# Units 6 and 7 of an attention-and-MLP kernel: transposes from TensorE to the DMA queue, loads issued behind them

## The chip, the cores and the metric

One core of a Trainium2 chip. The metric is the time of one execution in microseconds (us), the median over executions. Most executions of one kernel agree within 0.3%. All times inside a trace are microseconds from the start of the profiled span, and the span is about 1.7 us shorter than the time.

## The reference

A recurrent attention over 4 batches, 8 heads, 768 steps and a head width of 48; its output, as 3072 rows of 384, goes through two matrix layers with a SiLU between them.

```
for t in range(S):                                   # S = 768
    cur = einsum('bhd,bhe->bhde', u * k[t], v[t])
    y[t] = einsum('bhd,bhde->bhe', r[t], state + cur)
    state = w * state + einsum('bhd,bhe->bhde', k[t], v[t])
x = y as rows of (batch, step), columns of (head, d)   # 3072 x 384
h = x @ w_in                                           # 384 x 2048
out = (h * sigmoid(h)) @ w_out                         # 2048 x 384
```

## The kernel before

The sequence is cut into 6 chunks of 128 steps. A unit is one chunk of one batch, so there are 24 units: units 4 to 7 are chunk 1. Per unit, TensorE makes the scores (`p2`), the output y (`p3y`) and the state sums; VectorE adds the bonus term and writes y as 16-bit (`p3e`); `p4` turns y so that its columns lie on partitions, into xT, which layer one reads. Layers one and two (`l1`, `l2`) are cut into pieces, "fillers", and `fill(n)` puts some of them between the attention steps, so that TensorE always has work. Each engine runs its instructions in the order in which they are written.

```python
def p4(i):                                   # before
    ...
    if i >= 2 * B:                           # units 8 to 23: DMA transpose on the SyncE queue
        nc.sync.dma_start_transpose(out=xts[sc][:, :, b, :], in_=L["y16"]...)
        return
    yT = ps.tile(...)                        # units 0 to 7: three TensorE transposes,
    for q in range(NQ):
        nc.tensor.transpose(yT[:, q, :], yf[:, 128*q:128*q + 128], ident16)
    nc.scalar.copy(out=xts[sc][:, :, b, :], in_=yT)    # and a ScalarE copy out of PSUM

for i in range(B + 2, NU):                   # units 6 to 23; B = 4, NIN = 6
    ...                                      # p2(i), fill(2), front(i + 1)
    if NIN <= i < 2 * B:
        load(i + NIN)                        # i = 6, 7: loads of units 12, 13
    fill(1)
    p3y(i); p3e(i)
    ...                                      # sums, state
    fill(2)
    p4(i)
    if i >= 2 * B:
        load(i + NIN)
    ...
    fill(1)
    ...
    if b == B - 1:                           # after unit 7:
        if sc == 1:
            fillers.extend(l1s(1, 2, 4) + l2s(1))   # layer one over units 6 and 7
```

`load` issues three DMAs (r, k, v; 192 KB each) on the SyncE queue, the same queue that carries the DMA transposes and the output stores.

Of the kernel before, what the change touches and what calls it, by code (L numbers as in the profile page):

```python
# [15 lines left out]
def kernel(  # L16
# [13 lines left out]
    B, H, S, D = r.shape  # L30
# [10 lines left out]
    NIN = 6  # L41
# [19 lines left out]
    def unit(i):  # L61
        return divmod(i, B)

    def load(i, mid=None):
        if i >= NU:
            return
        sc, b = unit(i)
        for t, src in ((rin, r), (kin, k), (vin, v)):
            if t is vin and mid:
                mid()  # L70
            nc.sync.dma_start(out=t[i % NIN][:, :, 0:D],
                              in_=src[b, :, sc * C:sc * C + C, :]
                              .rearrange("h t d -> t h d"))
# [120 lines left out]
    def bonus_sum(i):  # L194
        L = live[i]
        L["rku"] = wrk.tile([128, H], FP, name="rku", bufs=3)
        nc.vector.tensor_reduce(out=L["rku"], in_=L["rku_f"], axis=mybir.AxisListType.X,  # L197
                                op=ALU.add)

    def bonus_vu(i):  # L200
        L = live[i]
        L["vu"] = wrk.tile([128, H, D], FP, name="vu", bufs=3)
        nc.gpsimd.tensor_tensor(out=L["vu"], in0=vin[i % NIN],  # L203
                                in1=L["rku"].unsqueeze(2).broadcast_to([128, H, D]),
                                op=ALU.mult)
# [50 lines left out]
    def r16(i):  # L256
        L = live[i]
        L["rT16"] = wrk.tile([PR, NP, C], F16, name="rT16")
        nc.scalar.copy(out=L["rT16"], in_=L["rT"])  # L259

    def p2(i, spins=0, nxt=None, late=False):
        L = live[i]
        ae = ps.tile([128, NP, C], FP, name="ae", tag="t", bufs=5)
        ao = ps.tile([128, NP, C], FP, name="ao", tag="t", bufs=5)
        spin(spins, ae)
        for p in range(NP):
            nc.tensor.matmul(ae[:, p, :], L["kT"][0:D, p, :], L["rT"][0:D, p, :],  # L267
                             start=True, stop=True)
            nc.tensor.matmul(ao[:, p, :], L["kT"][64:PR, p, :], L["rT"][64:PR, p, :],  # L269
                             start=True, stop=True)  # L270
        if nxt is not None:
            p1t(nxt)
        L["am"] = []
        for a in (ae, ao):
            am = wrk.tile([128, NP, C], F16, name="am", bufs=4)
            nc.vector.tensor_tensor(out=am, in0=a,  # L276
                                    in1=maskM.unsqueeze(1).broadcast_to([128, NP, C]),
                                    op=ALU.mult)
            L["am"].append(am)
        if nxt is not None and not late:  # L280
            p1d(nxt)

    def p3y(i):
        sc, b = unit(i)
        L = live[i]
        v16 = L["v16"]
        L["y"] = y = ps.tile([128, H, D], FP, name="y", tag="t", bufs=5)
        for p in range(NP):
            if sc:
                nc.tensor.matmul(y[:, 2 * p:2 * p + 2, :], L["rT16"][:, p, :],  # L290
                                 st16[b][:, p, :], start=True, stop=False)
            for j in range(2):
                nc.tensor.matmul(y[:, 2 * p + j, :], L["am"][j][:, p, :],  # L293
                                 v16[:, 2 * p + j, :], start=not sc,
                                 stop=(not sc or j == 1))

    def p3e(i):
        L = live[i]
        L["y16"] = wrk.tile([128, H, D], F16, name="y16", bufs=3)
        nc.vector.tensor_tensor(out=L["y16"], in0=L["y"], in1=L["vu"], op=ALU.add)  # L300

    def sums(i):
        sc, b = unit(i)
        L = live[i]
        L["sps"] = sps = ps.tile([128, NP, PW], FP, name="sps", tag="t", bufs=5)
        kf = kc[i % NKC].rearrange("p h d -> p (h d)")
        vf = L["v16"].rearrange("p h d -> p (h d)")
        for p in range(NP):
            nc.tensor.matmul(sps[:, p, :], kf[:, 128 * p:128 * p + 128],  # L309
                             vf[:, PW * p:PW * p + PW], start=True, stop=True)  # L310

    def state(i):
        sc, b = unit(i)
        sps = live[i]["sps"]
        for p0, c0 in ((0, 0), (64, D)):
            dst = st[b][p0:p0 + D, :, c0:c0 + D]
            if sc:
                nc.vector.tensor_tensor(out=dst, in0=sps[p0:p0 + D, :, c0:c0 + D],  # L318
                                        in1=sdec[b][p0:p0 + D, :, c0:c0 + D], op=ALU.add)
            else:  # L320
                nc.vector.tensor_copy(out=dst, in_=sps[p0:p0 + D, :, c0:c0 + D])
        if sc > 1:
            nc.gpsimd.tensor_copy(out=st16[b], in_=st[b])  # L323
        if sc < NCH - 2:
            nc.gpsimd.tensor_tensor(out=sdec[b], in0=st[b],  # L325
                                    in1=wCT.unsqueeze(2).broadcast_to([PR, NP, PW]),
                                    op=ALU.mult)

    def half_state(b):
        nc.scalar.copy(out=st16[b], in_=st[b])  # L330
# [3 lines left out]
    def p4(i):  # L334
        sc, b = unit(i)
        L = live[i]
        if sc not in xts:
            xts[sc] = wrk.tile([128, NQ, B, C], F16, name="xT", bufs=3)
        if i >= 2 * B:
            nc.sync.dma_start_transpose(out=xts[sc][:, :, b, :],  # L340
                                        in_=L["y16"].rearrange("p h d -> p (h d)"))
            return
        yT = ps.tile([128, NQ, C], F16, name="yT", tag="t", bufs=5)
        yf = L["y16"].rearrange("p h d -> p (h d)")
        for q in range(NQ):
            nc.tensor.transpose(yT[:, q, :], yf[:, 128 * q:128 * q + 128], ident16)  # L346
        nc.scalar.copy(out=xts[sc][:, :, b, :], in_=yT)
# [43 lines left out]
    def l1s(sc, b0=0, b1=B):  # L391
        return [((b1 - b0) / B, lambda ft=ft: l1(sc, ft, b0, b1)) for ft in range(NFT)]

    def l2s(sc, b0=0, b1=B):
        return [(1.0, lambda b=b, part=part: l2(sc, b, part))
                for b in range(b0, b1) for part in range(4)]
# [4 lines left out]
    def fill(n):  # L401
        owed[0] = min(owed[0] + n, n + 1.0)
        while fillers and owed[0] > 0.01:
            w_, f = fillers.pop(0)
            owed[0] -= w_
            f()
# [48 lines left out]
    p3e(1)  # L455
    spin(1)
    p4(0)
    p1(2)
    nat_ku(2)
# [5 lines left out]
    load(B)  # L465
    load(B + 1)
    p4(1)
    nc.scalar.copy(out=st[2], in_=zero)
    spin(2)
# [9 lines left out]
    p1(3)  # L479
    fill(1)  # L480
    p4(2)
    nat_ku(3)
    nat_rk(3)
# [20 lines left out]
    def front(i):  # L504
        nat_v(i)
        nat_ku(i)
        nat_rk(i)
        nat_kc(i)
# [63 lines left out]
    for i in range(B + 2, NU):  # L572
        sc, b = unit(i)
        if i == B + 2:
            p2(i, nxt=i + 1)
        bonus_sum(i)
        bonus_vu(i)
        if i > B + 2:
            p2(i, nxt=i + 1 if i + 1 < NU else None)
        fill(2)  # L580
        if i + 1 < NU:
            front(i + 1)
        if NIN <= i < 2 * B:
            load(i + NIN)
        fill(1)
        p3y(i)
        p3e(i)
        if sc < NCH - 1:
            sums(i)
            state(i)  # L590
        fill(2)
        p4(i)
        if i >= 2 * B:
            load(i + NIN)
        if i + 1 < NU:
            r16(i + 1)
        if i == B + 2:
            half_state(3)
        fill(1)
        if sc == 1:  # L600
            half_state(b)
        fill(1 if sc in (2, 3) else 2)
        if b == B - 1:
            if sc == 1:
                fillers.extend(l1s(1, 2, 4) + l2s(1))
            else:
                fillers.extend(l1s(sc) + l2s(sc))
# [32 lines left out]
```

## Time and profile before

| | before |
|---|---|
| time, median of 3 | 199.74 us (199.5 to 199.87) |
| profiled span | 197.8 us |
| TensorE busy | 189.7 us, 96% |
| DMA transposes | 16, median 2.4 us from issue to landing |
| granted TensorE clock | 1.000 |

The page gives the busy shares and the DMA load over the span; the timeline of one engine gives each group of instructions as start, duration, engine, source line, operation, output<-input, count, and in brackets how long the engine stood idle before it and what ended that. The lines that matter are in the prediction. Three more are needed later, all TensorE: the layer-one pieces just before unit 6's transposes, the start of layer two behind them, and the layer-two pieces just before the tile that the prediction calls the deadline.

```profile
45.53 1.47 PE L358 MATMUL hps<-xT,win 128*128 128x256 f16 x12
...
48.35 1.46 PE L370 MATMUL ops<-wout,gT 128*128 128x384 f16 x8
...
61.37 2.11 PE L370 MATMUL ops<-wout,gT 128*128 128x384 f16 x12
```

From 61.37 to the deadline tile at 63.32 are 1.95 us for twelve matmuls. There is no wait in it, so 1.95 us is the yardstick for that stretch in every other trace.

### The profile page before, as it was taken

To read this page: it belongs to the slowest core of one execution; us is meant where nothing else is said; L and a number is where in the kernel's file an instruction comes from. 1 tells how busy PE (TensorE), PEld (TensorE's weight loads), DVE (VectorE), ACT (ScalarE), POOL (GpSimd) and SP (SyncE) were. 2 spreads that over 40 slices of the span, in tenths; PEclk is the share of its full clock that TensorE was granted. 3 is DMA by queue.
4 is the path that set the end of the run, shared out by engine and by line. 5 is a ranking of instruction groups with operands and counts; after the bars stand their busy time and mean duration, and the time that the engine had idled before them with its cause. 6 is when DMAs were issued, how large, how long until landed. Compare 5 with 4: busy or idle time off the path is not lost.

```text
span 197.8 us, 4932 instructions
## 1 busy us (share of the span) xinstructions
PE 189.7 (96%) x1925; PEld 127.2 (64%) x1925; DVE 115.4 (58%) x233; ACT 91.9 (46%) x209; POOL 115.1 (58%) x145
## 2 busy tenths in 40 slices
PE   7889999998999999999999999999999999999993
PEld 2657878787766976675566766557656556544562
DVE  6687658885758746975575686466576344210121
ACT  3565487798232652215961216682015680069300
POOL 4499959979956795697669647735537710000000
PEclk9999999999999999999999999999999999999999
DMA  4999998999899883766456387520321011310022
GB/s 85 209 185 171 198 227 167 166 187 195 162 193 215 209 168 84 171 137 157 91 119 139 99 182 159 103 59 5 101 60 43 20 22 43 97 42 0 3 80 81
DMA packets 88864, 23.92 MB, mean 121 GB/s; under 512 B 82056, under 2 KB 88840, under 8 KB 88840
## 3 DMA queue, kind: packets, MB, share of 16 engines
q1 hardware_dynamic: 85160, 20.46, 48.0%
q0 software_dynamic: 3680, 3.15, 10.8%
q8 instruction: 15, 0.25, 0.5%
q14 instruction: 9, 0.07, 0.1%
HBM read 20.45 MB, written 4.72 MB: 127 GB/s over the span
## 4 chain that ended last, share of the span: by engine, by line
PE 82%; issue 5%; POOL 5%; DVE 4%; ACT 2%; POOLq 0%; DVEq 0%
PE ops L370 31%; PE hps L358 27%; PE ae L267 10%; PE xs L242 4%; PE y L293 3%; DVE am L276 2%; PE y L290 2%; POOL ku L180 2%; PE ops L384 1%; PE sps L309 1%; POOL rku_f L186 1%; PE yT L346 1%; ACT gT L361 1%; DVE y L300 1%; PE ao L269 1%
## 5 line engine op out<-in xcount | busy, mean ns | idle before, releaser
L361 ACT ACTIVATE gT<-hps 128x256 f16<-128x256 f32 (+1 forms) x128 | 59.7, 493 | 46.7 <-PE hps L358 45.0
L358 PE MATMUL hps<-xT,win 128*128 128x256 f16 (+1 forms) x384 | 69.4, 326 | 0.5 <-ACT gT L361 0.3
L370 PE MATMUL ops<-wout,gT 128*128 128x384 f16 x368 | 64.0, 327 | 0.0
L358 PEld LDWEIGHTS <-win 128*128 128x128 f16 x384 | 35.4, 98 | 23.3 <-issue 1.2
L370 PEld LDWEIGHTS <-gT 128*128 128x128 f16 x368 | 34.5, 98 | 22.3
L276 DVE TENSOR_TENSOR am<-ae,maskM 128x512 f16<-128x512 f32 x24 | 16.6, 691 | 36.2 <-PE ao L269 36.2
L374 DVE COPY osb<-ops 128x384 f32<-128x384 f32 x23 | 12.7, 554 | 27.5 <-PE ops L370 27.4
L267 PE MATMUL ae<-rk 48*128 48x128 f32 x192 | 27.7, 285 | 0.7 <-DVE rk L230 0.7
L267 PEld LDWEIGHTS ae<-rk 48*128 48x128 f32 x192 | 23.1, 187 | 8.1 <-issue 4.5
L269 PE MATMUL ao<-rk 48*128 48x128 f32 x192 | 27.7, 285 | 0.0
L259 ACT CAST rT<-rk 112x512 f16<-112x512 f32 x20 | 12.3, 616 | 32.1 <-DVE rk L253 32.1
L203 POOL TENSOR_TENSOR vu<-vin,rku 128x384 f32<-128x384 f32 x23 | 19.1, 830 | 13.8 <-DVE rku L197 13.7
L253 DVE TENSOR_TENSOR rk<-xs,pif 112x512 f32<-112x512 f32 x40 | 25.6, 681 | 1.7 <-PE xs L242 1.7
L186 POOL TENSOR_TENSOR rku_f<-rin,ku 128x384 f32<-128x384 f32 x24 | 24.1, 1006 | 1.9
L180 POOL TENSOR_TENSOR ku<-kin,u_bc 128x384 f32<-128x384 f32 x24 | 24.1, 1005 | 1.5 <-DMA kin<-in_k_dram 1.5
L191 POOL TENSOR_TENSOR kc<-kin,lamC 128x384 f16<-128x384 f32 x24 | 24.1, 1004 | 0.0
L269 PEld LDWEIGHTS ao<-rk 48*128 48x128 f32 x192 | 23.2, 187 | 0.0
L323 POOL CAST stb<-st 112x384 f16<-112x384 f32 x12 | 6.0, 503 | 22.2 <-DVE st L318 22.2
L300 DVE TENSOR_TENSOR y<-y,vu 128x384 f16<-128x384 f32 x24 | 13.4, 557 | 7.6 <-PE y L293 3.2
L276 DVE TENSOR_TENSOR am<-ao,maskM 128x512 f16<-128x512 f32 x24 | 16.3, 680 | 0.0
L325 POOL TENSOR_TENSOR sdec<-st,pif 112x384 f32<-112x384 f32 x16 | 13.3, 836 | 1.8 <-ACT gT L361 1.1
L197 DVE TENSOR_REDUCE rku<-rku_f 128x8 f32<-128x384 f32 x24 | 13.2, 549 | 2.0 <-POOL rku_f L186 1.6
(74 smaller groups left out, 171.0 us busy)
## 6 DMA issues: line engine op xcount, KB each, us to landing
rin<-in_r_dram SPq DMA_DIRECT2D x24, 192.0 KB, 3.6
kin<-in_k_dram SPq DMA_DIRECT2D x24, 192.0 KB, 3.4
vin<-in_v_dram SPq DMA_DIRECT2D x24, 192.0 KB, 3.6
out_dram<-osb SPq DMA_DIRECT2D x23, 192.0 KB, 1.9
win<-in_moe_w_in_dram POOLq DMA_DIRECT2D x4, 384.0 KB, 5.7
wout<-in_moe_w_out_dram POOLq DMA_DIRECT2D x2, 768.0 KB, 11.3
xT<-y SPq DMA_TRANSPOSE x16, 2.4
out_dram<-osh SPq DMA_DIRECT2D x1, 128.0 KB, 1.8
```

The source lines that it names most:

```text
L180: nc.gpsimd.tensor_tensor(out=L["ku"], in0=kin[i % NIN][:, :, 0:D], in1=u_bc, op=ALU.mult)
L186: nc.gpsimd.tensor_tensor(out=L["rku_f"], in0=rin[i % NIN][:, :, 0:D], in1=L["ku"], op=ALU.mult)
L191: nc.gpsimd.tensor_tensor(out=kc[i % NKC][:, :, 0:D], in0=kin[n][:, :, 0:D], in1=lamC, op=ALU.mult)
L203: nc.gpsimd.tensor_tensor(out=L["vu"], in0=vin[i % NIN], in1=L["rku"].unsqueeze(2).broadcast_to([128, H, D]), op=ALU.mult)
L253: nc.vector.tensor_tensor(out=rk[:, :, :, 64 * g:64 * g + 64], in0=xs[g][0:PR], in1=lam(g), op=ALU.mult)
L267: nc.tensor.matmul(ae[:, p, :], L["kT"][0:D, p, :], L["rT"][0:D, p, :], start=True, stop=True)
L269: nc.tensor.matmul(ao[:, p, :], L["kT"][64:PR, p, :], L["rT"][64:PR, p, :], start=True, stop=True)
L276: nc.vector.tensor_tensor(out=am, in0=a, in1=maskM.unsqueeze(1).broadcast_to([128, NP, C]), op=ALU.mult)
L300: nc.vector.tensor_tensor(out=L["y16"], in0=L["y"], in1=L["vu"], op=ALU.add)
L358: nc.tensor.matmul(hps, win[:, q, ft * 128:(ft + 1) * 128], xts[sc][:, q, b0:b1, :].rearrange("p b t -> p (b t)"), start=(q == 0), stop=(q ...
L361: nc.scalar.activation(out=gts[sc][:, ft, b0 * C:b1 * C], in_=hps, func=AF.Silu)
L370: nc.tensor.matmul(ops, gts[sc][:, ft, b * C:(b + 1) * C], wout[:, ft, :], start=(ft == 0), stop=(ft == NFT - 1))
```

## The change

The intent is to take two units' transposes off the engine that is full. Their slot loads go behind the transposes on the queue, so that the transposes need not stand behind them.

```diff
@@ p4
-        if i >= 2 * B:
+        if i >= NIN:
             nc.sync.dma_start_transpose(...)
@@ the loop over units 6 to 23
-        if NIN <= i < 2 * B:
-            load(i + NIN)
         fill(1)
         p3y(i)
...
         p4(i)
-        if i >= 2 * B:
+        if i >= NIN:
             load(i + NIN)
```

## The prediction

> **What bounds the kernel now.** I read the page from the top: busy shares, then the slices, then the chain. All times are microseconds from the start of the profiled span.
>
> ```profile
> span 197.8 us, 4932 instructions
> PE 189.7 (96%) x1925; PEld 127.2 (64%) x1925; DVE 115.4 (58%) x233; ACT 91.9 (46%) x209; POOL 115.1 (58%) x145
> ...
> PE   7889999998999999999999999999999999999993
> ...
> DMA  4999998999899883766456387520321011310022
> ...
> PE 82%; issue 5%; POOL 5%; DVE 4%; ACT 2%; POOLq 0%; DVEq 0%
> ```
>
> TensorE is busy 96% of the span and is 82% of the chain that ended last, so a microsecond gained or lost in TensorE's own order is gained or lost at the end, unless a later wait swallows it. The DMA row is full over the first third (slices of 4.95 us, so up to about 70 us). That is where the change lies: units 6 and 7 are the third and fourth units of the second chunk (units 4 to 7), at about 42 to 57 us. So I read the timeline of each engine from 38 to 66 us. First TensorE, at the two transposes that go, and at the first layer-one matmul behind the second layer of chunk 0:
>
> ```profile
> 47.52 0.34 PE L346 MATMUL yT<-ident,y 128*128 128x128 f16 x3 [0.51 <-DVE y L300]
> 47.70 0.82 PE L358 MATMUL hps<-xT,win 128*128 128x256 f16 x6
> ...
> 55.10 0.33 PE L346 MATMUL yT<-ident,y 128*128 128x128 f16 x3
> 55.27 2.11 PE L370 MATMUL ops<-wout,gT 128*128 128x384 f16 x12
> ...
> 63.32 0.82 PE L358 MATMUL hps<-xT,win 128*128 128x256 f16 x6
> ```
>
> What to see: unit 6's transposes hold TensorE for 0.51 us waiting for VectorE's y, then take 0.18 us of issue (47.52 to 47.70). Unit 7's come without a wait and take 0.17 us (55.10 to 55.27). The chain of waits also runs through here: from 40.65 to 47.52 it goes over POOL and the VectorE addition, the last place but two short ones before the end where TensorE waits for another engine.
>
> The row at 63.32 is the deadline. By the source, the work pushed at the end of unit 7 is layer one of chunk 1 for units 6 and 7, and it stands behind layer one for units 4 and 5 and all of layer two of chunk 0. The 256-wide rows at 63.32 are its first two tiles. They read both units' columns of xT, so **both transposes must have landed by then**.
>
> Now the queue on which the new transposes are issued:
>
> ```profile
> 52.95 0.75 SPq L71 DMA_DIRECT2D rin<-in_r_dram  x1
> 53.80 0.74 SPq L71 DMA_DIRECT2D kin<-in_k_dram  x1
> 54.63 0.67 SPq L71 DMA_DIRECT2D vin<-in_v_dram  x1
> 55.41 0.84 SPq L71 DMA_DIRECT2D rin<-in_r_dram  x1
> 56.33 1.81 SPq L71 DMA_DIRECT2D kin<-in_k_dram  x1
> 58.24 0.72 SPq L71 DMA_DIRECT2D vin<-in_v_dram  x1
> 59.06 0.60 SPq L376 DMA_DIRECT2D out_dram<-osb  x1
> 59.77 0.37 SPq L71 DMA_DIRECT2D rin<-in_r_dram  x1
> ...
> 63.87 1.31 SPq L340 DMA_TRANSPOSE xT<-y  x1
> ```
>
> Counting the triples from the start, the one at 52.95 loads unit 11, 55.41 unit 12, 59.77 unit 13; 63.87 is the transpose of unit 8. The queue issues without a gap: it is in arrears. Unit 12's load is written before unit 6's matmuls end, at about 45 us, yet issues at 55.41. The arrears come from 36 to 50 us, when unit 9's three loads took 5.23, 4.84 and 3.58 us to issue beside the weight transfer of 768 KB.
>
> **What the Trainium skill says.** "VectorE: DVE Perf Modes", section "The three transpose paths", lists 390 ns on TensorE against 1309 ns by DMA for a 128x128 16-bit transpose. The trace agrees in direction only: a TensorE transpose here shows 219 to 231 ns, and in a stream three of them cost 0.17 us; a DMA transpose of three such blocks shows 1.18 to 1.82 us of issue and 2.3 to 4.5 us to landing. So the DMA path is longer, but costs TensorE nothing unless awaited. "DMA: Bandwidth & Descriptors", section "Anatomy of one DMA", says that a DMA's semaphore wait happens on the issuing sequencer before dispatch. The listing agrees: on this queue a DMA that is not ready, or an issue that is slow, delays all behind it. "Perfetto Trace Analysis", section "Identifying the Most-Contended Engine", warns that matmul busy share is no measure of the distance to the peak. It applies: the weight loads are at 64%. Hence I count TensorE's gains by distances between starts and not by the busy times of 0.33 us.
>
> **The change part by part.**
>
> Removed from TensorE: 0.51 + 0.18 us at unit 6, 0.17 us at unit 7, sum 0.86 us. It is on the path, and I see no wait that takes its place between 47 and 62 us: the layer-two weights' second half, issued at 37.78 with 12.3 us to landing, is there at 50.1 against a use at about 50.6 (51.28 less 0.69); the masked scores of unit 7 are ready at 52.22 against a use at 53.25, and move with TensorE. So the deadline moves from 63.32 to 62.46.
>
> Removed from ScalarE: two copies at 0.48 us. Beside other work: in this stretch it waits 4.7 us before one of them. Worth nothing. Also two of the rotating PSUM buffers' uses go; no TensorE wait here is for one.
>
> Added on the queue, unit 6: its y is ready at 47.46, but its place is behind unit 11's load, so it issues at about 55.4, for 1.3 us (like unit 8's), and lands by 58 to 60, well before 62.46. It pushes everything behind it. If issue time binds, by 1.3 us; if DMA throughput binds, by its bytes: 96 KB at the 0.2 MB/us of this stretch, about 0.5 us.
>
> Added, unit 7: its y is ready at 54.46, earlier by 0.69 with TensorE. Its place is behind unit 12's load and the first output store, because the load of unit 12 moves only just behind unit 6's transpose. Those two end at 59.67 now, so it issues at 59.67 + 0.1 + (0.5 to 1.3) = 60.2 to 61.0. Time to landing: unit 8's, in the same traffic, shows 2.7; unit 9's, behind a congested load, 4.5. So it lands between 62.9 and 65.5, most likely 63.2 to 64.5. Against 62.46 that is a **new TensorE wait of 0.4 to 3.0 us, about 1.3**.
>
> Moved: the loads of units 12 and 13, later by about 1 to 3 us. Unit 12 is turned at about 85 us and unit 13 later, over 20 us after landing. Worth nothing. Unit 8's transpose and the stores move by 2 to 3 us, and unit 8's is not read until chunk 2's layer one at 87.65.
>
> Sum: -0.86 + 1.3 = +0.4 us. The new wait lies inside the stretch where TensorE is otherwise full, so later work does not absorb it, save perhaps 0.2 us at 70.88, where TensorE now waits 0.28 us for ScalarE. I put the time at **200.1 us**.
>
> **The rivals.**
>
> Hidden anyway: if unit 7's transpose lands before 62.46, only the gain remains, 199.74 - 0.86 = 198.9 us. For it: the queue may be limited by throughput, and the issue of 1.81 us at 56.33 has slack that the transpose might use. Against it: the arithmetic above reaches 62.9 at best.
>
> Long wait: crowded DMA engines give the 4.5 us landing and the queue slips by the full 1.3 us or more: wait 3 us, time 202 us. For it: the DMA row is at 9 in these slices and some issues on the queue take 1.8 us or more. Against it: unit 8's 2.7 us right behind a load and two stores.
>
> False dependency: unit 6's transpose writes a tile whose other columns TensorE is still reading, at 47.70. If the order were kept for the whole tile, TensorE would stand from 47 to 58 us, 11 us, and the time would be near 210 us. Against it: in the trace the matmuls from 47.70 to 48.52 run over the ScalarE copy into the same tile (47.90 to 48.38), so columns are told apart.
>
> Nearer the weight landing: if the waits of POOL come back, TensorE gains less than 0.69 at unit 6, which costs up to half a microsecond.
>
> **Range and chances.** Hidden anyway has about 0.25, the middle case 0.55, the long wait 0.17, the false dependency 0.03. That gives a range from 198.8 to 201.8 us, with 0.2% between executions. Two per cent is 4 us; only the false dependency or an unforeseen stall reaches it. Faster by over 2% would need 4 us out of parts that hold 0.86.
>
> **What would show each step.** The 0.51 us gap before unit 6's transposes is gone and layer one goes on at about 47.0. There are 18 DMA transposes; the first issues at about 55.4, the second at 60 to 61. At about 62.5 the first 256-wide layer-one tile behind layer two waits for the DMA transpose, 0.4 to 3 us; this is the step I am least sure of. No wait for loads appears near 85 us. The prediction is wrong if the first transpose issues much before or after 55.4, if TensorE waits between 47 and 62 us for something new, or if the later layers lose or gain time that this account does not hold.

## The result, and the profile after

| | before | after |
|---|---|---|
| time, median of 6 each | 199.52 us (199.26 to 199.87) | 198.93 us (198.31 to 199.31) |
| ratio | | 0.9963 (0.9941 to 0.9984) |
| profiled span | 197.8 us | 197.4 us |

A ratio here and below is the mean time of one kernel's fast runs over that of the other's of the same rounds, so not quite the ratio of the medians. Where I turn a ratio into microseconds I multiply its distance from 1 by the median of before in those rounds: here -0.74 us, interval -1.18 to -0.32. The change made the kernel slightly faster, where the prediction had it 0.36 us slower.

The page of the changed kernel:

```profile
span 197.4 us, 4920 instructions
...
PE 190.3 (96%) x1919; PEld 127.8 (65%) x1919; DVE 115.5 (59%) x233; ACT 91.0 (46%) x207; POOL 115.0 (58%) x145
...
PE 83%; DVE 5%; issue 4%; POOL 3%; ACT 1%; DMA 1%; POOLq 0%; DVEq 0%
```

TensorE's busy time did not fall although six transposes left it: a reminder that this sum measures overlapping windows. The new entry is DMA in the chain, 1%. The TensorE timeline shows where it comes from:

```profile
45.80 2.13 PE L358 MATMUL hps<-xT,win 128*128 128x256 f16 x18
47.76 1.46 PE L370 MATMUL ops<-wout,gT 128*128 128x384 f16 x8
...
60.62 2.11 PE L370 MATMUL ops<-wout,gT 128*128 128x384 f16 x12
63.23 0.81 PE L358 MATMUL hps<-xT,win 128*128 128x256 f16 x6 [0.50 <-DMA xT<-y]
```

At the top, the twelve and six layer-one matmuls that unit 6's transposes had parted now run as one group of 18. The start of that group to the start of layer two is 1.96 us, against 2.82 us before (45.53 to 48.35): **0.86 us gained**. At the bottom, the deadline tile starts 2.61 us after its predecessor, 0.66 us over the yardstick: **the new wait**. The bracket says 0.50 because the profile counts idle time from the modelled end of the last matmul. The queue:

```profile
54.20 0.75 SPq L71 DMA_DIRECT2D vin<-in_v_dram  x1
55.05 1.74 SPq L340 DMA_TRANSPOSE xT<-y  x1
56.89 0.51 SPq L71 DMA_DIRECT2D rin<-in_r_dram  x1
57.49 0.54 SPq L71 DMA_DIRECT2D kin<-in_k_dram  x1
58.14 1.61 SPq L71 DMA_DIRECT2D vin<-in_v_dram  x1
59.84 0.85 SPq L376 DMA_DIRECT2D out_dram<-osb  x1
60.78 1.20 SPq L340 DMA_TRANSPOSE xT<-y  x1
```

Unit 6's transpose issues at 55.05, then unit 12's load, one store, and unit 7's transpose at 60.78. TensorE goes on 2.45 us after that issue, at 63.23.

### The profile page after: what moved, and what is told of

The parts are those of the page before. It is cut to its first block, busy times and chain, and to the rows that moved or that the text cites. A ratio compares the mean times of both kernels' runs of the same rounds, so it can differ in the third digit from the quotient of the medians.

```text
span 197.4 us, 4920 instructions
## 1 busy us (share of the span) xinstructions
PE 190.3 (96%) x1919; PEld 127.8 (65%) x1919; DVE 115.5 (59%) x233; ACT 91.0 (46%) x207; POOL 115.0 (58%) x145
## 4 chain that ended last, share of the span: by engine, by line
PE 83%; DVE 5%; issue 4%; POOL 3%; ACT 1%; DMA 1%; POOLq 0%; DVEq 0%
PE hps L358 30%; PE ops L370 29%; PE ae L267 11%; PE xs L242 4%; PE y L293 3%; DVE am L276 2%; PE y L290 2%; PE sps L309 1%; PE ops L384 1%; DMA xT<-y 1%; POOL rku_f L186 1%; POOL ku L180 1%; ACT gT L361 1%; PE yT L346 1%; PE ao L269 1%
```

## The experiments

Theory A: TensorE's gain is what the starts show (0.86 us at unit 6, 0.17 us at unit 7), less a wait for unit 7's transpose that its place on the queue makes. Theory B: executions as a rule have no such wait and the first trace was an accident. Theory C: the transpose's own landing makes the wait, wherever it stands. Every run of the eleven gave correct results.

To compare traces that start differently, I use three starts in each: the first scores of unit 4 (30.10 us in before), the deadline tile (63.32) and the last VectorE copy (194.58). "Middle" is the distance from the first to the second, less before's 33.22 us. "End" is from the last copy to the end of the span, which the trace gives to a thousandth (197.847 in before). What lies between the tile and the last copy takes 131.26 or 131.27 us in every trace of the account below, so nothing is lost or gained there. The stretch before unit 4's scores is left out: the program is the same there in every kernel, and it scatters from 29.82 to 30.74 us.

### The changed kernel again, and the place of the loads

No edit in the first run.

> The changed kernel once more, for a second trace and a narrower interval. Theory A (gain counted by starts, 0.86 us at unit 6 and 0.17 us at unit 7, less a wait for unit 7's DMA transpose that varies from execution to execution): 0.3 to 0.8 us faster than before, and a TensorE wait for the DMA transpose of 0.2 to 1.0 us in this trace. Theory B (the wait in the first trace was an accident, and executions as a rule have none): about 1.0 us faster, and no such wait.

198.99 us, ratio 0.9956 (0.9936 to 0.9975), -0.88 us. The profiled execution was a freak of 489 us and gives no trace: TensorE's layer-two matmuls took a mean of 687 ns there, against 326 ns in the first trace. It was the only such execution, and is left out of the ratio; its cause stays open. The other five lie between 198.26 and 199.20 us. For traces, two more looks were taken:

> The changed kernel, one look for another trace (the trace of the last repeat fell on an execution of 489 us). Theory A: TensorE waits for unit 7's DMA transpose by 0.2 to 1.0 us between starts at the first 256-wide layer-one tile behind layer two; the transpose issues at 60 to 61.5 us. Theory B (no wait as a rule): no such wait.

> The same as again2, once more: both looks together say whether the wait of the first trace was an accident. Theory A: a wait again, of a size that differs by some tenths of a microsecond.

The TensorE timelines around the deadline tile, again2 and then again3:

```profile
60.28 2.11 PE L370 MATMUL ops<-wout,gT 128*128 128x384 f16 x12
62.91 0.81 PE L358 MATMUL hps<-xT,win 128*128 128x256 f16 x6 [0.52 <-DMA xT<-y]
```

```profile
60.14 2.11 PE L370 MATMUL ops<-wout,gT 128*128 128x384 f16 x12
63.15 0.81 PE L358 MATMUL hps<-xT,win 128*128 128x256 f16 x6 [0.90 <-DMA xT<-y]
```

The waits by starts are 0.68 and 1.06 us (2.63 and 3.01 less 1.95). All three traces of the changed kernel have the wait, a mean of 0.80 us, so Theory B is out as a rule. (A single look has no fast or slow state on record; both times, 198.87 and 199.10 us, lie among the fast runs.) Unit 7's transpose issued at 60.45 and 60.44.

Next, both loads behind the second transpose:

```diff
         p4(i)
-        if i >= NIN:
+        if i == NIN + 1:
+            load(2 * NIN)
+        if i > NIN:
             load(i + NIN)
```

> The changed kernel with the loads of units 12 and 13 both put behind unit 7's transpose on the queue. Theory A: the place on the queue makes the wait, so unit 7's transpose issues at about 57 to 58 us, lands before 61, TensorE waits for no DMA transpose, and the time is 1.0 us under before and 0.3 to 0.7 us under the changed kernel. Theory B: same time as the changed kernel within 0.2 us.

198.15 us, ratio 0.9922 (0.9906 to 0.9938), -1.56 us. Its queue and its deadline tile:

```profile
54.36 1.35 SPq L340 DMA_TRANSPOSE xT<-y  x1
55.80 0.52 SPq L376 DMA_DIRECT2D out_dram<-osb  x1
56.41 1.56 SPq L340 DMA_TRANSPOSE xT<-y  x1
```

```profile
60.08 2.11 PE L370 MATMUL ops<-wout,gT 128*128 128x384 f16 x12
62.02 0.82 PE L358 MATMUL hps<-xT,win 128*128 128x256 f16 x6
```

The transpose issues 4 us sooner and the distance is 1.94 us: the wait is gone. **This version beats both kernels**, the changed one by 0.7 us (0.9922 over 0.9956). Unit 12's load moved on the queue and nothing else, so the queue's order makes the wait. The total is 0.5 us better than the expected -1.0; the end of the program explains most of that, below.

The opposite, both loads ahead as in before:

```diff
+        if NIN <= i < 2 * B:
+            load(i + NIN)
         fill(1)
 ...
-        if i >= NIN:
+        if i >= 2 * B:
             load(i + NIN)
```

> Both units turned by DMA, but the loads of units 12 and 13 at their places of before, ahead of the transposes. Theory A: unit 7's transpose stands behind one more load of three issues, some 2 to 3 us, issues at 63 to 64 us and lands at 65.5 to 66.5, so TensorE waits 3 to 4 us for it and the time is 2 to 3 us above before. Rival C (the transpose's own landing time, not the queue, makes the wait): the wait stays near 0.7 us and the time stays under before.

204.41 us, ratio 1.0208 (1.0161 to 1.0254), +4.2 us.

```profile
60.70 2.11 PE L370 MATMUL ops<-wout,gT 128*128 128x384 f16 x12
66.18 1.46 PE L358 MATMUL hps<-xT,win 128*128 128x256 f16 x6 [3.37 <-DMA xT<-y]
```

The transpose issues at 63.24 and TensorE waits 3.5 us by starts, as expected; Theory C is out. But the time, expected 2 to 3 us above before, rose by more than the wait less the gain (3.5 - 1.0). The windows show why (columns: window, its length, busy time of TensorE, its weight loads, VectorE, ScalarE and POOL with counts, granted TensorE clock, DMA share, GB/s):

```profile
64.00:66.00 2.00, 0.00 (x0) 0.00 (x0) 0.00 (x0) 0.00 (x0) 1.85 (x3) 0.82 0.96 200
66.00:68.00 2.00, 1.82 (x10) 1.16 (x12) 0.00 (x0) 0.70 (x2) 1.89 (x2) 0.50 0.73 226
68.00:70.00 2.00, 2.00 (x28) 2.00 (x28) 0.31 (x1) 0.07 (x1) 0.00 (x0) 0.50 0.61 119
70.00:72.00 2.00, 2.00 (x18) 1.44 (x15) 2.00 (x4) 0.44 (x2) 0.00 (x0) 0.50 1.11 263
72.00:74.00 2.00, 2.00 (x31) 1.81 (x30) 0.32 (x2) 1.90 (x6) 0.00 (x0) 0.97 0.04 12
```

The granted clock falls to one half at about 65.3 us, just before the wait ends at 66.18, and stays there until about 72 us. The shortfall against full clock, summed and doubled, is 6.8 us at half speed. The Trainium skill, "TensorE: Matmul & The Clock Gate", section "What's actually happening", describes this: the clock of TensorE is halved after an idle window of about 3.4 us, on a window that runs freely. 6.8 us is two such windows. No execution was spared, but there are two kinds: four of 203.97 to 204.99 us at a mean clock of 0.981 to 0.983, and two of 202.18 and 202.28 us at 0.991. A dose between, with two of unit 13's three loads ahead of unit 7's transpose:

```diff
-        p4(i)
-        if i >= NIN:
-            load(i + NIN)
+        if i == NIN + 1:
+            load(i + NIN, mid=lambda: p4(i))   # r and k, then p4, then v
+        else:
+            p4(i)
+            if i >= NIN:
+                load(i + NIN)
```

> The changed kernel with two of the three loads of unit 13 ahead of unit 7's transpose on the queue. Theory A: the transpose issues 1.2 to 1.8 us later than in the changed kernel, TensorE waits about 2 us by starts, no clock drop follows (the wait of 3.5 us in the run with a whole load ahead was followed by a stretch at a granted clock of 0.50), and the time is 1.0 to 1.8 us above the changed kernel. If the clock drops after 2 us as well, 3 us or more above it.

202.1 us, ratio 1.0083 (1.0036 to 1.0129). The expectation of no clock drop missed.

```profile
64.75 0.82 PE L358 MATMUL hps<-xT,win 128*128 128x256 f16 x6 [2.44 <-DMA xT<-y]
```

The wait by starts was 2.60 us (the layer-two group starts at 60.20, the tile at 64.75), and the clock fell: 0.91, 0.50 and 0.73 in the windows from 64 to 70 us, which is 3.4 us at half speed, from about 65.6 us, when TensorE was already at work again. The stretch from the tile to the last copy shows the cost: 132.85 us here and 134.03 in loads_ahead, against 131.26 at full clock, so 1.6 and 2.8 us. The six executions fall into two kinds: 199.79 and 199.96 us at a mean clock of 1.000, and four of 202.02 to 202.76 us at 0.991 to 0.992. So a wait of under 3 us can bring a halved clock and cost 1.6 us more than itself. Whether the same wait can also go without is not shown: the two quicker executions left no trace, and from this trace's middle and end (as in the account below) a wait of 2.60 us at full clock would give about 201.0 us, so theirs was probably a microsecond shorter (an estimate).

### The two units apart

Unit 6 alone by DMA (unit 7 by TensorE), and unit 7 alone:

```diff
-        if i >= NIN:                     # in p4
+        if i == NIN or i >= 2 * B:       # only6
+        if i > NIN:                      # only7
```

> Only unit 6 turned by DMA, unit 7 by TensorE as before; loads as in the changed kernel. Theory A: no wait for a DMA transpose is left, 0.86 us faster than before. If the gain at unit 6 is the 0.69 us of the prediction (the idle time that the profile lists plus the issue), 0.69 us. Theory B (no wait as a rule in the changed kernel): 0.17 us slower than the changed kernel.

198.54 us, ratio 0.9941 (0.9924 to 0.9958), -1.18 us. No wait for a DMA transpose, and the middle is 0.86 us shorter, as the starts had it and not the 0.69 us of the prediction. Half of the change is at least as good as the whole: 0.9941 against 0.9956 in the same rounds, with intervals that overlap.

> Only unit 7 turned by DMA, unit 6 by TensorE as before, loads as in the changed kernel. Theory A: the transpose of unit 7 comes without one ahead of it, so it issues at about 59 to 60 us and lands at 61.5 to 62.7, before TensorE asks for it at about 63.15: no wait, and a gain of 0.17 us over before, not told from 0 by the times. Rival: unit 7's transpose waits however the queue stands, and the time is 0.5 us or more above before.

199.38 us, ratio 0.9987 (0.9974 to 1.0000), -0.26 us. The transpose issued at 61.17 in a trace that starts 0.64 us late (unit 4's scores at 30.74), so at 60.5 by before's start, no sooner than in the changed kernel. The expected 59 to 60 us was wrong: the issue of unit 12's k load took 2.62 us there, against 0.54 us behind the transpose in the changed kernel. What one slow issue takes, another may give back, so what unit 6's transpose costs the queue can't be told from these traces. The transpose landed 2.8 us after its issue, at 64.0, and TensorE went on at 64.05: it waited about 0.25 us by starts (61.85 to 64.05, less 1.95), though the profile lists no wait and none was expected.

Is it the transposes or the wait before them? Unit 6's stay on TensorE, one piece of layer one later:

```diff
-        p4(i)
+        if i != B + 2:
+            p4(i)
 ...
         fill(1)
+        if i == B + 2:
+            p4(i)
```

> The kernel before without any DMA transpose added: unit 6's three TensorE transposes come one piece of layer one (six matmuls, 0.65 us) later. Theory A: TensorE's gain at unit 6 was for 0.68 us of waiting for y and only 0.18 us of transposes, so this alone brings 0.65 us, the time is 0.6 to 0.7 us under before, and the wait of the transposes for VectorE falls from 0.5 to under 0.1 us. Rival: the gain needs the transposes off TensorE, and the time stays within 0.2 us of before.

199.03 us, ratio 0.9967 (0.9955 to 0.9979), -0.66 us, as expected. Its timeline:

```profile
45.56 2.13 PE L358 MATMUL hps<-xT,win 128*128 128x256 f16 x18
47.55 0.34 PE L346 MATMUL yT<-ident,y 128*128 128x128 f16 x3
47.73 1.46 PE L370 MATMUL ops<-wout,gT 128*128 128x384 f16 x8
```

No bracket before the transposes: y is ready when their turn comes. Four fifths of what unit 6 gave was a wait, and a move of a line takes it away without any DMA.

### The end of the program

A copy of the kernel before:

> The kernel before, sent as an experiment, for a second trace of it and the noise of a ratio. Theory A: ratio 1.000 within 0.003; the start of the first scores of unit 1 (17.54 us in the first trace) and the stretch from the last VectorE copy to the end (3.27 us) scatter by 0.3 us from execution to execution. If instead both stay as they were, the traces of the changed kernels differ from before by something in the first 20 us or at the end that the account by starts has left out.

199.72 us, ratio 0.9999 (0.9987 to 1.0011). The start does scatter (30.32 against 30.10), but the end does not: 3.26 us against 3.27. So the ends of the changed kernels, 0.3 us shorter, needed a cause. The order of the queue's instructions has a lead: each DMA there signals its landing on one of eight semaphores (counters that an engine can wait on), taken in turn. The last two stores take numbers 1 and 2 of 0 to 7 in before, 3 and 4 in the changed kernel, because two transposes were added. Two small loads that nothing reads shift the turn equally:

```diff
+        if i == NU - NIN:          # unit 18
+            load_row(wrow, w)
+            load_row(urow, u)
```

> The kernel before with two loads of 1.5 KB added on the queue at unit 18, which nothing reads. They shift by two the rotation of the eight semaphores that the queue's transfers take in turn, as the two added transposes do in the changed kernel. If the shorter end of the changed kernels (2.94 us from the last VectorE copy to the end, against 3.27 to 3.34 us in the traces without added transposes) comes from that rotation, this one ends in 2.9 to 3.0 us as well and is 0.3 us faster than before. If it comes from the transposes themselves or from TensorE, the end stays at 3.3 us and the time at that of before.

199.26 us, ratio 0.9982 (0.9968 to 0.9995), -0.36 us, with no change on TensorE. The queue's own waits at the end, before, the changed kernel and this run (who waited <- for whom: us in total, times, longest):

```profile
SPq L635 <- DMA out_dram<-osh: 1.3, 2, 0.6
```

```profile
SPq L633 <- DMA out_dram<-osh: 0.9, 2, 0.5
```

```profile
SPq L638 <- DMA out_dram<-osh: 0.9, 2, 0.5
```

The wait for the last stores is 0.4 us shorter with the shifted turn. The last store lands 1.5 us after issue in both shifted kernels, 1.7 us in before.

That two more DMAs on the queue shorten the end is shown. That it is the semaphores' turn is shown for a part only. The packed traces also hold SyncE's last waits: it goes through the eight semaphores in a fixed order, about 0.06 us for each that is already there. The last store's is the third in before, so five follow it, and the fifth in the changed kernel, so three follow: 0.12 of the 0.33 us. With one DMA added (only6 and only7) the end lies between, at 3.02 and 3.01 us. Most of the rest is that the last store lands sooner; why is not settled.

### The account

| kernel | middle, us | end, us (before 3.27) | sum against before, us | measured, us |
|---|---|---|---|---|
| changed, first trace | -0.35 | 2.94 | -0.68 | -0.74, again -0.88 |
| changed, again2 | -0.34 | 2.95 | -0.66 | one look |
| changed, again3 | +0.05 | 2.96 | -0.26 | one look |
| loads_behind | -1.02 | 2.94 | -1.35 | -1.56 |
| only6 | -0.86 | 3.02 | -1.11 | -1.18 |
| only7 | +0.09 | 3.01 | -0.17 | -0.26 |
| pe_later | -0.66 | 3.31 | -0.62 | -0.66 |
| two_small | +0.01 | 2.95 | -0.31 | -0.36 |
| before_copy | +0.01 | 3.26 | 0.00 | -0.02 |

Example for loads_behind: 62.02 - 29.82 = 32.20, less 33.22 is -1.02; the end adds 2.94 - 3.27 = -0.33. Each sum lies within the interval of its kernel's measured value, but for again3, whose -0.26 lies outside; the mean of the three traces of the changed kernel is -0.53. Where the wait for the transpose is longest (again3), the change is worth nothing on TensorE and only the end is left.

## Why the prediction was wrong

The measured 198.93 us lies in the range, but the direction was wrong: the sum said -0.86 + 1.3 = +0.4 us. The mechanism was right: TensorE gains, and a new wait for unit 7's transpose takes part of it back. The sizes were not: three terms were off, all toward too slow.

- **The wait, "about 1.3" us**, measured 0.66, 0.68 and 1.06. This is the step that failed most. The place on the queue was right (predicted issue 60.2 to 61.0; 60.78, 60.45, 60.44), and so was the deadline (predicted 62.46; 62.57, less the 0.26 us by which that trace starts late, is 62.31). What failed was the time to landing: "2.7" to "4.5" us from two transposes of before, while from issue to TensorE's next start the three traces show 2.45, 2.46 and 2.71 us. The 2.7 was the top of what occurred at this place on the queue, not the bottom. Weighting in unit 9's 4.5 us was the mistake here: that one stood behind a load that took 5.5 us to land. The range as such was not absurd: at other places unit 7's transpose took 2.8 (only7), 2.9 (loads_ahead) and 3.3 us (half_ahead) to land, and unit 6's 3.1 to 4.8. What sets this time is not shown.
- **The gain, "0.51 + 0.18"**, measured 0.86. The text said it would count by distances between starts and then took 0.51 from the idle bracket, which begins at a modelled end. By starts it was to be had from before: 45.53 to 48.35 is 2.82 us; without the transposes the pieces take 1.96 us, as the changed kernel shows. Unit 7's 0.17 us was right: loads_behind has both and shows 1.02 us, only6 0.86 us.
- **The end was missing**: 0.33 us, which the two added DMAs bring. The prediction did not look at the end of the program.

With the measured terms: -1.03 + 0.80 - 0.3 is -0.5 us, inside the measured interval of -1.18 to -0.32. The wait alone put right gives -0.06 us, wait and gain -0.23: it takes all three to reach the interval.

Right were: TensorE's order as the bound, the deadline at the first tile over units 6 and 7, no load waited for near 85 us, no false dependency, ScalarE's copies worth nothing. The rival "hidden anyway" named 198.9 us, close to the result, but for the wrong reason: the wait is there in every trace. "Long wait" counted a wait of 3 us as 3 us; the two runs with loads ahead show that it may bring a halved clock with it, worth 1.6 to 2.8 us.

## What to carry to other kernels

Work taken off a full engine and put on a queue is worth what it saves less the wait for it, and the queue's order sets that wait: put first what is needed first, here both transposes ahead of loads that nobody reads for 20 us. Before moving an operation to another engine, see how much of its cost is a wait for its input; a later place in the order may save that at no cost. Count gains by the distances between starts, and test differences of a few tenths of a per cent against a run that changes nothing but the number of DMAs.

## What the Trainium skill lacked or had wrong

- "TensorE: Matmul & The Clock Gate", section "🎯 Why this matters for your kernels", advises against TensorE gaps of more than about 3 us, and the section quoted above names a whole idle window of 3.4 us. In loads_ahead the clock fell about 2.5 us after the last matmul before the wait had ended (60.70 + 2.11, a modelled end). In one trace of half_ahead a wait of 2.60 us was followed by 3.4 us at a granted clock of 0.50, and four of six executions of that kernel, this one among them, show the same mean clock, 0.991 to 0.992. Waits of 0.7 to 1.1 us left the clock at 1.00 in that stretch.
- "VectorE: DVE Perf Modes", section "The three transpose paths", gives 390 ns on TensorE against 1309 ns by DMA for one 128x128 block. In a full stream three TensorE transposes cost 0.17 us; a DMA transpose of three blocks took 2.3 to 4.8 us from issue to landing beside loads. Neither figure says what a move between the two is worth.
- No page that I read has the effect of the number of DMAs on a queue on the end of the program: 0.3 us shorter from two loads of 1.5 KB, of which 0.12 us goes with the place of the last store's semaphore among the eight that SyncE waits for at the end.
